# An attention pair on one core: one output group per 16 steps at a fixed place in the loop, with VectorE's small work put beside it

## The chip, the cores and the metric

The kernel runs on one core of one Trainium2 chip. What counts is the device time of that core in microseconds (us); three runs before the change gave 1822.85, 1823.55 and 1823.87 us.

## The reference

Two attention blocks over 2048 positions with 640 features and 32 heads of 20 are computed independently, and their outputs stand side by side. A looks back at 8 positions, two apart; B is full attention.

```python
def _A_ref(x, wqkv, wo):                 # H = 32, Dh = 20, W = 8, dil = 2
    ...
    q, k, v = qkv[0], qkv[1], qkv[2]
    ...
    logits = jnp.einsum("bhsd,bhswd->bhsw", q, kg) * scale
    logits = jnp.where(mask[None, None, :, :], logits, -1e9)
    attn = _softmax(logits, axis=-1)
    o = jnp.einsum("bhsw,bhswd->bhsd", attn, vg)
    return (lambda x, *d: x.transpose(*d))(o, 0, 2, 1, 3).reshape(B, S, D) @ wo

def _B_ref(x, wqkv, wo):
    ...
    scores = jnp.einsum("bhqd,bhkd->bhqk", q, k) * (Dh ** -0.5)
    p = _softmax(scores, axis=-1)
    o = jnp.einsum("bhqk,bhkd->bhqd", p, v)
    return (lambda x, *d: x.transpose(*d))(o, 0, 2, 1, 3).reshape(B, S, D) @ wo

return jnp.concatenate([a, b], axis=-1)
```

## The kernel before

The program has three stages. First TensorE makes the projections of A and B. Then comes **the loop**, which is most of the time: B's attention, with A's attention threaded through it. Last come 24 steps without maxima and B's output projection, which I call **the tail**.

**B's loop** has 512 steps (`NS`). A step is one block of 128 keys against 512 queries of four heads; 16 steps (`NKB`) make a unit, and four units a group of four heads. Per step there are four score matmuls (`s`, 512 columns, contraction 62), whose results ScalarE turns into exponentials (`e`), and four more matmuls (`m`) that give the scores transposed, from which VectorE takes row maxima (`mx`). The maxima run 24 steps (`LEAD`) ahead of the scores, so the first 488 steps have both kinds and the last 24 have scores alone. Then a step's four `P` matmuls (`e` times `vb`) add into one bank of PSUM; two steps share a bank, and ScalarE copies it out (`more`), for GpSimd to add into `braw`.

Two steps make a **pair**, written out by hand in `b_pair`, always two score or maximum matmuls at a time, in two row halves of the array. In the words of the new code the order of a pair is `P sm MM ss P sm MM ss sm sm`: `MM` are two maxima that one VectorE instruction reads (1024 elements), `sm` a score and a maximum (512 elements). So a pair has two reductions of 1024 and four of 512 on VectorE, and eight exponentials and one copy on ScalarE.

**PSUM** has eight banks, which every kind of matmul shares inside the loop. A planner chooses the bank: `pe`, `act` and `dve` carry running estimates of time (`.us`), `read_at[n]` says when bank `n` will have been read, and `b_two`, `b_pv` and `bank` take the bank that is free first by that. It decides which bank, not the order of the work.

**The other work** is queued by `after(n, fn)`, which runs `fn` n steps later, in `tick`. Every engine runs its instructions in the order in which they were written. On VectorE the small work of the loop is:

- `max_rows`: the last reduction of a unit's maxima (`mx<-mx`) and its transpose (`mtr`);
- `normalize`: a reciprocal of the sums (`sm`), which come from SyncE's DMAs `s_d<-braw` and `sm<-s_d`, and go back through `s_d<-sm` and `rb<-s_d`;
- `a_softmax`: a maximum (`am<-al`) and a reciprocal (`am<-am`) for each of A's 16 tiles of 128 rows;
- `a_turn`: five transposes (`turn<-ao`) for each tile of A's result.

**A's attention** is 128 pieces (`UNITS`), mostly on GpSimd; `next(a_work)` does one. 23 of them stand ahead of the loop. In the loop `i % 30 % 4 == 1` takes eight in 30 steps. A's **output groups** (`a_out`: 15 matmuls `ww,aot` of 320 columns and one copy `ro`; two per tile, 32 in all) are started by `out_piece` at every sixth step, between the halves of a pair, if one is ready. B's own output groups (`out_group`, 15 matmuls `ww,xn`/`ww,xl`) for all but the last quarter of the queries wait in the list `fill`, which is popped once per pair.

The lines that do this in the loop:

```python
        if i > 14 and i % 30 % 4 == 1 and next(a_work, 0) == 0:
...
        if done_a and done_a[0][0] <= 0 and i % 8 == 7 and i > 14:
            a_turn(*done_a.pop(0)[1:])
...
        if fill:
            fill.pop(0)()
        elif i % 6 == 5 and not out_piece() and not left_a[0] and not WO_b:
            load_out(wo_b, WO_b)
```

Nearly all instructions are recorded by one helper, so that the profile gives them one line, L60; they are told apart by their tiles.

Of the kernel before, what the change touches and what calls it, by code (L numbers as in the profile page):

```python
# [12 lines left out]
ALU = mybir.AluOpType  # L13
AX = mybir.AxisListType
# [7 lines left out]
KC = 5  # L22
# [18 lines left out]
NKB = 16  # L41
# [23 lines left out]
def attention_pair(ctx, tc, xa, wqk_a, wv_a, wo_a, xb, wqk_b, wv_b, wo_b, oa, ob):  # L65
# [14 lines left out]
        due.setdefault(now[0] + n, []).append((fn, args))  # L80

    loop = [None]

    def odd(n):

# [10 lines left out]
    pair = [0]  # L96
    taken = {}
    read_at = []

    def bank():  # L100

        if read_at:
            n = one(pe.us)
            pe.us = max(pe.us, read_at[n]) + 2.2
# [245 lines left out]
    def a_scores(t, c, kv):  # L350
# [7 lines left out]
            pool(kv[:, :, :n], kv[:, :, :n], kv[:, :, n:2 * n], ALU.add)  # L358
        pool(L[:, 2 * c:2 * c + 2], kv[:, :, :H], kv[:, :, 4 * H:5 * H], ALU.add)

    def a_softmax(t):

        _, L, _ = a_t[t]
        if t % (NT // 2) == 0:
            pool(L, L, mask, ALU.add)
        yield
        yield
        m = sb.tile([128, 4, H], F32, tag="am", bufs=2, name="am")
        dve.tensor_reduce(m[:, 0], L.rearrange("p o h -> p h o"), AX.X, ALU.max)
        yield  # L370
        pool(L, L, m[:, 0].unsqueeze(1).to_broadcast([128, WIN, H]), ALU.subtract)
        yield
        yield
# [5 lines left out]
        yield  # L379
        dve.reciprocal(m[:, 0], m[:, 0])  # L380
        yield
        pool(L, L, m[:, 0].unsqueeze(1).to_broadcast([128, WIN, H]), ALU.mult)

    def a_values(t, c, kv):
# [15 lines left out]
    def a_attention():  # L400
        for n in range(2):
            a_fetch(n)
        soft = {}
        for n, (t, c) in enumerate(UNITS):
            a_fetch(n + 2)
            for g in soft.values():
                next(g, None)
            if c == 4:
                for _ in soft.pop(t):
# [12 lines left out]
            next_a[0] = n + 1  # L422
            yield
# [165 lines left out]
    def max_rows(m4, m1, q, qc):  # L589
# [2 lines left out]
        md = dr.tile([2, GH * 512], F32, tag="mdr", bufs=4, name="mdr")  # L592
        raw = mt[:, 0].bitcast(F32)

        def turn():

            dve.transpose(raw, m1)
# [13 lines left out]
        t = odd(1)  # L611
        after(t, dve.tensor_reduce, m1[:, :16], m4.rearrange("p r a c -> p (r a) c"), AX.X, ALU.max)
        after(t, turn)
        after(t + 1, parts)
        after(t + 3, store)
        after(t + 4, load)

    def normalize(raw, g, c0, t, then):

        sm = sb.tile([128, 16], F32, tag="sm", bufs=2, name="sm")  # L620
        s_d = dr.tile([2, GH, 512], F32, tag="s_d", bufs=4, name="s_d")
        rb = sb.tile([128, 512], F32, tag="rb", bufs=2, name="rb")

        def bcast():
            for j in range(GH):
                sp.dma_start(rb[32 * j:32 * j + 32], s_d[1, j].partition_broadcast(32))

        def out():
            for j in range(GH):
                r0 = (g * GH + j) * DH  # L630
                sp.dma_start(ot_b[r0:r0 + DH, c0:c0 + 512], raw[32 * j:32 * j + DH])
        after(t, sp.dma_start, s_d[0], raw[DH:128:32])
# [3 lines left out]
        after(t + 1, sp.dma_start, s_d[1].rearrange("j (p c) -> j p c", c=16), sm)  # L636
        after(t + 2, bcast)
        after(t + 4, pool, raw, raw, rb, ALU.mult)
        after(t + 8, out)
        if then:  # L640
            after(t + 9, then)

    mxt = {}
    m1s = [sb.tile([128, 32], F32, tag=f"mx1{n}", bufs=1, name="mx1") for n in range(2)]
# [1 line left out]
        gp.memset(t, 0.0)  # L646

    def max_tiles(i):
        u, sub = divmod(i, NKB)
        if sub == 0:  # L650
# [14 lines left out]
    def max_end(i):  # L665
        u, sub = divmod(i, NKB)
        if sub == NKB - 1:
            max_rows(*mxt[u], stacks[u // NQC][0], u % NQC)

    def b_max(i):  # L670
# [39 lines left out]
                    give(ps2[r])  # L710

    exp_at = {}
    behind_v = [False]

    def b_pv(i):
        u, kb = divmod(i, NKB)
# [37 lines left out]
    def b_two(what):  # L754

        t = pe.us + 0.129 * behind_v[0]
        lag = 0.53 if behind_v[0] else 0.44
# [30 lines left out]
    def b_pair(i, pv):  # L788

        m = i + LEAD  # L790
        max_tiles(m)
        s = [("s", i + j, pl, r) for j in range(2) for pl in range(2) for r in range(2)]
        pv(i - LAG)
        b_two([s[0], ("m", m, 0, 1)])
        b_two([("m", m, 1, 0), ("m", m, 1, 1)])
        b_two([s[1], s[2]])
        yield
        pv(i - LAG + 1)
        b_two([s[3], ("m", m, 0, 0)])
        b_two([("m", m + 1, 0, 0), ("m", m + 1, 0, 1)])  # L800
        yield
        b_two([s[4], s[5]])
        b_two([s[6], ("m", m + 1, 1, 1)])
        b_two([s[7], ("m", m + 1, 1, 0)])
        max_end(m + 1)


    outs_b = {}
# [48 lines left out]
        after(1, sp.dma_start, vb_d[s * 128:(s + 1) * 128, half * 16 * VC:half * 16 * VC + c], ve[:, :c])  # L857


    V_GROUPS = [(n, half, s) for n in (2, 3, 0, 1) for half in range(2) for s in range(4 * n, 4 * n + 4)]  # L860
    v_late = V_GROUPS[-LAG:]
    for n, half, s in V_GROUPS[:-LAG]:
# [16 lines left out]
            next(a_work, None)  # L879
        if groups in (26, 28):  # L880
            v_piece(0, *((0, 4) if groups == 26 else (8, 16)))
    tick()
    after(4, v_piece, 0, 4, 8)
    wait[0] = 2
    WO, loads = [], []

    def load_out(src, W, halves=range(2)):
        for h in halves:
            w, more = wide_pieces(src[h], gp)
            W.append(w)  # L890
            loads.extend(more)
    load_out(wo_a, WO, (0,))
    assert next(steps, None) is None


    outs = iter(())
# [12 lines left out]
    read_at += 8 * [0.0]  # L909
    for e in (pe, act, dve):  # L910
        e.us = 0.0
    for i in range(NS + LAG):
        g, sub = divmod(i, NQC * NKB)
        if sub == 4 and g + 1 < NG:
# [14 lines left out]
        if i + LEAD >= NS:  # L929

            read_at.clear()
            if i < NS:
                b_qk(i)
            if i % 2:
                b_pv(i - LAG - 1)
                b_pv(i - LAG)
                if fill:
                    fill.pop(0)()
            continue
        if i % 2 == 0:  # L940
            steps = b_pair(i, b_pv if i else lambda _: v_group(*v_late.pop(0)))
        next(steps)
        if i % 2 == 0:
            continue
# [4 lines left out]
        if fill:  # L949
            fill.pop(0)()  # L950
        elif i % 6 == 5 and not out_piece() and not left_a[0] and not WO_b:
            load_out(wo_b, WO_b)
        next(steps, None)


    qc = NQC - 1
# [54 lines left out]
```

## Time and profile before

| What | us |
|---|---|
| median of three runs | 1823.55 |
| the profiled execution: its span, from the first to the last instruction | 1820.8 |
| difference of the two | 2.75 |
| VectorE busy over the span | 1337.7 |
| ScalarE busy | 1327.9 |
| GpSimd busy | 1219.7 |
| TensorE busy with matmuls, as modelled | 1802.5 |

For the profiled execution no time is given beside its span, so the table sets the median of the runs against it. The loop's 244 pairs lie between 448.93 and 1711.27 us: I number them from 0 and let each begin with the start of its first maximum on VectorE. The granted clock of TensorE is 1.00 in every window of the loop and the tail.

### The profile page before, as it was taken

What the parts mean: (1) busy time and instruction counts of PE and PEld (TensorE: products, weight loads), DVE (VectorE), ACT (ScalarE), POOL (GpSimd) and SP (SyncE); (2) the same over time, 40 slices, a digit from 0 to 9 for tenths busy, and PEclk for the clock granted to TensorE, in tenths of its full rate; (3) what the DMA queues carried; (4) which work ended last, traced back from release to release, by engine and by line L of the source; (5) the groups of instructions that cost most, each with busy time, mean ns of one, the idle gap of its engine ahead of it and who ended that gap; (6) DMA issues with size and microseconds to landing.
All of it is one profiled execution on the core that took longest, in us unless ns stands there. A gap on an engine that the chain in (4) does not pass through costs nothing. (4 is left out here: it accounts for less than half of the span.)

```text
span 1820.8 us, 31714 instructions
## 1 busy us (share of the span) xinstructions
PE 1802.5 (99%) x11211; PEld 997.1 (55%) x11211; DVE 1337.7 (73%) x1838; ACT 1327.9 (73%) x2597; POOL 1219.7 (67%) x1072
## 2 busy tenths in 40 slices
PE   9999999999999999999999999999999999999999
PEld 8888888877344444444343444444444444443568
DVE  3100232357999999999999899999999999999400
ACT  4222322212998888998989889889998999899892
POOL 0000068856689889999989989899999973346232
PEclk9999999999999999999999999999999999999999
DMA  6323696874443444354435335353543441121023
GB/s 227 112 94 108 193 311 247 275 246 142 127 145 111 131 131 124 119 146 138 116 106 154 116 115 130 112 146 103 154 129 121 109 116 53 40 67 55 28 74 110
DMA packets 193015, 240.31 MB, mean 132 GB/s; under 512 B 90972, under 2 KB 121308, under 8 KB 191864
## 3 DMA queue, kind: packets, MB, share of 16 engines
q1 hardware_dynamic: 192280, 237.63, 43.1%
q8 instruction: 88, 1.44, 0.3%
q10 hardware_dynamic: 576, 0.66, 0.1%
q14 instruction: 71, 0.58, 0.1%
HBM read 173.29 MB, written 64.91 MB: 131 GB/s over the span
## 5 line engine op out<-in xcount | busy, mean ns | idle before, releaser
L60 DVE TENSOR_REDUCE mx<-ps_st 128x1 f32<-128x512 f32 (+1 forms) x1512 | 1216.0, 869 | 95.3 <-PE ps_st L60 92.1
L60 ACT ACTIVATE e<-ps_st 128x512 f32<-128x512 f32 x2048 | 1063.2, 611 | 54.6 <-PE ps_st L60 36.3
L60 PE MATMUL ps_st<-bq,bk 62*128 62x512 f32 x2048 | 629.4, 443 | 1.1 <-ACT e L60 0.5
L60 PE MATMUL ps_st<-bk,bq 60*128 60x512 f32 x2048 | 594.5, 441 | 7.5 <-DVE mx L60 4.2
L60 PEld LDWEIGHTS ps_st<-bq,bk 62*128 62x128 f32 x2048 | 286.1, 184 | 523.1 <-ACT e L60 296.7
L60 PE MATMUL ps_st<-e,vb 128*32 128x512 f32 x4096 | 542.9, 604 | 3.0 <-ACT e L60 2.8
L60 POOL TENSOR_TENSOR braw<-braw,more 128x512 f32<-128x512 f32 x224 | 287.6, 1284 | 199.6 <-ACT more L60 196.1
L60 POOL TENSOR_TENSOR akv<-akv,aq 128x1280 f32<-128x1280 f32 x64 | 189.0, 2953 | 239.5 <-DMA akv<-ka_d 239.5
L60 PEld LDWEIGHTS ps_st<-bk,bq 60*128 60x128 f32 x2048 | 273.6, 184 | 51.1 <-DVE mx L60 23.6
L60 POOL TENSOR_TENSOR akv<-akv 128x640 f32<-128x640 f32 (+3 forms) x304 | 284.5, 936 | 23.8
L60 ACT COPY ro<-ps_st 128x480 f32<-128x480 f32 (+1 forms) x124 | 61.3, 496 | 237.2 <-PE ps_st L60 182.7
L60 PEld LDWEIGHTS ps_st<-e,vb 128*32 128x32 f32 x4096 | 82.1, 108 | 159.4 <-issue 99.8
L60 POOL TENSOR_TENSOR akv<-akv,al 128x1280 f32<-128x1280 f32 x64 | 152.1, 2377 | 13.2 <-DMA bq<-qb_d 7.0
L60 PE MATMUL ps_st<-wc,xn 128*128 128x480 f32 x576 | 135.8, 380 | 0.2 <-ACT xn L60 0.2
L60 ACT COPY more<-ps_st 128x512 f32<-128x512 f32 x224 | 132.8, 593 | 2.0 <-PE ps_st L60 1.8
L60 PE MATMUL ps_st<-ww,xn 128*128 128x320 f32 x768 | 129.5, 319 | 1.6 <-ACT ww L60 1.1
L60 PEld LDWEIGHTS ps_st<-ww,xn 128*128 128x128 f32 x768 | 116.0, 192 | 23.3 <-ACT e L60 9.2
L60 PEld LDWEIGHTS ps_st<-wc,xn 128*128 128x128 f32 x576 | 107.9, 188 | 18.0 <-ACT xn L60 0.8
L60 PE MATMUL ps_st<-xn,w 128*128 128x512 f32 x480 | 115.8, 390 | 0.0
L60 PEld LDWEIGHTS ps_st<-xn,w 128*128 128x128 f32 x480 | 90.1, 188 | 19.3
L60 ACT CAST pr<-ps_st 128x512 fp32r<-128x512 f32 x40 | 23.6, 589 | 100.9 <-PE ps_st L60 100.9
L60 DVE TENSOR_TENSOR pr<-ps_st,pr 128x512 fp32r<-128x512 f32 x40 | 27.7, 692 | 91.4 <-ACT pr L60 91.4
(64 smaller groups left out, 995.8 us busy)
## 6 DMA issues: line engine op xcount, KB each, us to landing
akv<-ka_d SPq DMA_DIRECT2D x128, 320.0 KB
akv<-va_d SPq DMA_DIRECT2D x128, 320.0 KB
kb_d<-pr SPq DMA_DIRECT2D x20, 512.0 KB
qb_d<-pr SPq DMA_DIRECT2D x20, 512.0 KB
bk<-kb_d SPq DMA_DIRECT2D x16, 640.0 KB
bq<-qb_d SPq DMA_DIRECT2D x64, 160.0 KB
rb<-s_d SPq DMA_DIRECT2D x128, 64.0 KB
stg<-xb SPq DMA_DIRECT2D x12, 512.0 KB
```

The costliest lines, as they stand in the source:

```text
L60: return self.tc.keep_in_program_order(op(*a, **k))
```

## The change

The pair's order becomes data. `PAIR` is the order of before. `BESIDE` is used for one pair of eight, the one with `i % 16 == 8`; it begins with `G`, one of A's output groups ahead of the pair's own scores, and has its two `P` together. Right behind the group's matmuls `flush` writes all of VectorE's small work that has come due since the last such place (`beside`). After step 452 `G` does two groups. A's pieces come at `i % 4 == 3`, four in 16 steps. `a_turn` writes its five transposes together instead of one per step, and at most once per 16 steps. B's output groups are not taken inside the loop any more. The first tile of A is turned, and the first half of A's output weights loaded, ahead of the loop. `small` gives the planner a stated time for each small instruction, and `bank` counts the switch from `P`.

```diff
+    PAIR = "P sm MM ss P sm MM ss sm sm".split()
+    BESIDE = "G ss sm MM sm P P ss sm MM sm".split()
+    def b_pairs(pv, group):
+        scores = ((i, pl, r) for i in range(NS - LEAD) for pl in range(2) for r in range(2))
+        maxima = ((m, j) for m in range(LEAD, NS) for j in range(2))
...
+        for i in range(0, NS - LEAD, 2):
+            for t in BESIDE if i % NKB == NKB // 2 else PAIR:
+                if t == "P":
+                    yield
+                    pv(next(steps))
+                elif t == "G":
+                    group()
...
+    def small(us, op, *args):
+        t = dve.us
+        op(*args)
+        dve.us = t + us
...
+    def flush():
+        while beside:
+            op = beside.pop(0)
+            (small if len(op) > 1 else op[0])(*(op if len(op) > 1 else ()))
+    def group():
+        for _ in range(2 if now[0] - loop[0] > NS - 60 else 1):
+            out_piece()
+        flush()
...
         for k in range(KC):
-            after(1 + k, dve.transpose, b[:, k], o[:, k * 128:(k + 1) * 128])
-        after(KC + 2, sp.dma_start, d, b.rearrange("p k c -> p (k c)"))
-        after(KC + 5, back)
+            small(0.27, dve.transpose, b[:, k], o[:, k * 128:(k + 1) * 128])
+        after(2, sp.dma_start, d, b.rearrange("p k c -> p (k c)"))
+        after(5, back)
...
+        def turn():
+            small(0.24, dve.reciprocal, sm, sm)
+            after(1, sp.dma_start, s_d[1].rearrange("j (p c) -> j p c", c=16), sm)
+            after(2, bcast)
+            after(4, pool, raw, raw, rb, ALU.mult)
+            after(8, out)
...
-        t = odd(t + 3)
-        after(t, dve.reciprocal, sm, sm)
+        if now[0] - loop[0] < NS - LEAD - NKB // 2 - 4:
+            after(t + 3, beside.append, (turn,))
+        else:
+            after(t + 3, turn)
...
-            normalize(raws.pop(u), g, qc * 512, 2 if last else 5, (lambda: out_last(qc)) if last else None)
+            normalize(raws.pop(u), g, qc * 512, 2 if last else 3, (lambda: out_last(qc)) if last else None)
...
-        if i > 14 and i % 30 % 4 == 1 and next(a_work, 0) == 0:
+        if i > 14 and i % 4 == 3 and next(a_work, 0) == 0:
             for d in done_a:
                 d[0] -= 1
-        if done_a and done_a[0][0] <= 0 and i % 8 == 7 and i > 14:
-            a_turn(*done_a.pop(0)[1:])
+        if i % NKB == NKB // 2 - 1 and done_a and done_a[0][0] <= 0:
+            beside.append((lambda d=done_a.pop(0): a_turn(*d[1:]),))
...
+        if groups == 14:
+            a_turn(*done_a.pop(0)[1:])
```

VectorE, before, over some two pairs in the middle of the loop (`128x1` is a reduction of 512 elements, `128x2` one of 1024; the number behind `mx` is the buffer of one unit's maxima, and `mx_2531` the unit's last reduction):

```order
L60 TENSOR_REDUCE mx_4445<-ps_st 128x2
L60 TENSOR_REDUCE am<-al 128x32
L60 TENSOR_REDUCE mx_4445<-ps_st 128x1
L60 TENSOR_REDUCE mx_4445<-ps_st 128x2
L60 TENSOR_REDUCE mx_4445<-ps_st 128x1 x2
L60 TENSOR_REDUCE mx_4911<-ps_st 128x1
L60 TENSOR_REDUCE mx_4911<-ps_st 128x2
L60 RECIPROCAL sm<-sm 128x16
L60 TENSOR_REDUCE mx_2531<-mx_4445 128x16
L60 STREAM_TRANSPOSE mtr<-mx_2531 128x32
L60 TENSOR_REDUCE mx_4911<-ps_st 128x1
```

And after, at one of the new places:

```order
L60 TENSOR_REDUCE mx_4935<-ps_st 128x2
L60 TENSOR_REDUCE mx_4935<-ps_st 128x1 x2
L60 RECIPROCAL am<-am 128x32
L60 RECIPROCAL sm<-sm 128x16
L60 STREAM_TRANSPOSE turn<-ao 128x128 x5
L60 TENSOR_REDUCE mx_2532<-mx_4935 128x16
L60 STREAM_TRANSPOSE mtr<-mx_2532 128x32
L60 TENSOR_REDUCE mx_5388<-ps_st 128x1
L60 TENSOR_REDUCE mx_5388<-ps_st 128x2
```

The small work has moved into one block at the boundary between two units' maxima. These nine instructions stand there in every second block; in the others the block is `am<-al`, `sm<-sm`, `mx<-mx` and `mtr`, four instructions.

TensorE, before, around one of A's output groups (`bq,bk` are scores, `bk,bq` maxima, `e,vb` a `P`, `ww,aot` the group):

```order
L60 MATMUL ps_st<-e,vb 32x512 x4
L60 MATMUL ps_st<-bq,bk 128x512
L60 MATMUL ps_st<-bk,bq 128x512 x3
L60 MATMUL ps_st<-ww,aot 128x320 x15
L60 MATMUL ps_st<-bq,bk 128x512 x3
L60 MATMUL ps_st<-bk,bq 128x512
L60 MATMUL ps_st<-bq,bk 128x512
L60 MATMUL ps_st<-bk,bq 128x512
L60 MATMUL ps_st<-e,vb 32x512 x4
```

And after, around the same kind of group:

```order
L60 MATMUL ps_st<-bq,bk 128x512
L60 MATMUL ps_st<-bk,bq 128x512
L60 MATMUL ps_st<-ww,aot 128x320 x15
L60 MATMUL ps_st<-bq,bk 128x512 x3
L60 MATMUL ps_st<-bk,bq 128x512 x3
L60 MATMUL ps_st<-bq,bk 128x512
L60 MATMUL ps_st<-bk,bq 128x512
L60 MATMUL ps_st<-e,vb 32x512 x8
L60 MATMUL ps_st<-bq,bk 128x512 x3
L60 MATMUL ps_st<-bk,bq 128x512 x3
```

The group has moved from the middle of a pair to its head, and the pair's two `P` have come together behind its first four scores. The loop has 30 such places, eight pairs apart; the last two have two groups each (`x30`).

More of the change, by code (lines that the diff above doesn't have):

```diff
@@ L82, in attention_pair, with in_place @@
     loop = [None]
+    beside = []
+    def small(us, op, *args):
+        t = dve.us
+        op(*args)
+        dve.us = t + us
+    def in_place(n, *ops):
+        if loop[0] is None:
+            for op in ops:
+                after(n, small, *op)
+        else:
+            after(n, beside.extend, ops)
     def odd(n):
@@ L408, in a_attention @@
             if c == 4:
+                late.add(t)
                 for _ in soft.pop(t):
@@ L610, in load @@
                              md[:, r * 1024:(r + 1) * 1024].rearrange("t (p c) -> t p c", p=2))
[L611 to L616, printed above, removed]
+        def turn():
+            small(0.17, dve.tensor_reduce, m1[:, :16], m4.rearrange("p r a c -> p (r a) c"), AX.X, ALU.max)
+            small(0.21, dve.transpose, raw, m1)
+            after(1, parts)
+            after(3, store)
+            after(4, load)
+        if loop[0] is None:
+            after(1, turn)
+        else:
+            beside.append((turn,))
     def normalize(raw, g, c0, t, then):
@@ L857, in v_group, with load_out @@
         after(1, sp.dma_start, vb_d[s * 128:(s + 1) * 128, half * 16 * VC:half * 16 * VC + c], ve[:, :c])
+    WO, loads = [], []
+    def load_out(src, W, halves=range(2)):
+        for h in halves:
+            w, more = wide_pieces(src[h], gp)
+            W.append(w)
+            loads.extend(more)
     V_GROUPS = [(n, half, s) for n in (2, 3, 0, 1) for half in range(2) for s in range(4 * n, 4 * n + 4)]
@@ L881, in attention_pair @@
             v_piece(0, *((0, 4) if groups == 26 else (8, 16)))
+        if groups == 14:
+            a_turn(*done_a.pop(0)[1:])
+        turn_parts()
+        if groups == 28:
+            wait[0] = 2
+            load_out(wo_a, WO, (0,))
+        if loads and groups >= 28:
+            loads.pop(0)()
     tick()
     after(4, v_piece, 0, 4, 8)
[L884 to L893, printed above, removed]
+    assert next(steps, None) is None and not loads
     outs = iter(())
@@ L911, in attention_pair @@
         e.us = 0.0
+    def flush():
[6 more added lines that the diff above has]
+        flush()
+    steps = b_pairs(lambda i: b_pv(i) if i >= 0 else v_group(*v_late.pop(0)), group)
+    next(steps)
     for i in range(NS + LAG):
@@ L948, in attention_pair @@
             spare += [sb.tile([128, 2, 512], F32, tag="last0", bufs=2, name="more") for _ in range(2)]
[L949 to L953, printed above, removed]
+        if i < NS - LEAD:
+            next(steps, None)
+            if not left_a[0] and not WO_b:
+                load_out(wo_b, WO_b)
+            continue
+        read_at.clear()
+        flush()
+        if i < NS:
+            b_qk(i)
+        if i % 2:
+            b_pv(i - LAG - 1)
+            b_pv(i - LAG)
+            if fill:
+                fill.pop(0)()
     qc = NQC - 1
```

121 lines of the change are left out of this document (65 added, 56 removed).

## The prediction

> **What bounds the kernel now.** I read the page's first part, then the windows over the loop, then VectorE's groups of instructions in the loop, then who waits for whom, and last single pairs.
>
> ```profile
> PE 1802.5 (99%) x11211; PEld 997.1 (55%) x11211; DVE 1337.7 (73%) x1838; ACT 1327.9 (73%) x2597; POOL 1219.7 (67%) x1072
> 448.93:1711.27 1262.34, 1253.12 (x8335) 543.21 (x8332) 1191.43 (x1661) 1139.91 (x2245) 1018.85 (x888) 1.00 0.40 114
> ```
>
> The second row is the loop: 1262.34 us, then the busy time of PE, PEld, DVE, ACT and POOL. VectorE (DVE) is busy for 1191.43 us, 94%; ScalarE (ACT) for 1139.91 us. The loop is bound by VectorE, with 71 us in which it stands still. VectorE's work there, and its waits:
>
> ```profile
> L60 DVE TENSOR_REDUCE mx<-ps_st 128x1 f32<-128x512 f32 x972 | 627.6, 679 | 66.7 <-PE ps_st L60 63.5
> L60 DVE TENSOR_REDUCE mx<-ps_st 128x2 f32<-128x1024 f32 x486 | 590.6, 1215 | 0.0
> L60 DVE STREAM_TRANSPOSE turn<-ao 128x128 f32<-128x128 f32 x80 | 23.4, 293 | 0.0
> L60 DVE TENSOR_REDUCE am<-al 128x32 f32<-128x256 f32 x13 | 7.9, 610 | 0.0
> L60 DVE RECIPROCAL sm<-sm 128x16 f32<-128x16 f32 x30 | 7.2, 240 | 0.0
> L60 DVE STREAM_TRANSPOSE mtr<-mx 128x32 f32<-128x32 f32 x30 | 6.3, 212 | 1.2
> L60 DVE TENSOR_REDUCE mx<-mx 128x16 f32<-128x64 f32 x31 | 5.2, 169 | 0.0
> L60 DVE RECIPROCAL am<-am 128x32 f32<-128x32 f32 x13 | 4.2, 326 | 1.1 <-POOL am L60 1.1
> DVE mx L60 <- PE ps_st L60: 65.5, 81, 1.9
> ACT ro L60 <- PE ps_st L60: 66.0, 35, 2.5
> L60 ACT COPY ro<-ps_st 128x320 f32<-128x320 f32 x35 | 15.0, 427 | 66.0 <-PE ps_st L60 66.0
> ```
>
> Two things matter here. The small work (the last six DVE rows) is 23.4 + 7.9 + 7.2 + 6.3 + 5.2 + 4.2 = 54.2 us. And VectorE's 65.5 us of waiting for TensorE belong to the output groups: ScalarE waits 66.0 us for its 35 copies `ro`, one behind each group (32 of A's, so 3 of B's). One such place:
>
> ```profile
> 833.79 2.47 PE L60 MATMUL ps_st<-ww,aot 128*128 128x320 f32 x15
> 836.30 0.43 ACT L60 COPY ro<-ps_st 128x320 f32<-128x320 f32 x1 [1.90 <-PE ps_st L60]
> 836.99 1.29 DVE L60 TENSOR_REDUCE mx<-ps_st 128x1 f32<-128x512 f32 x2 [1.48 <-PE ps_st L60]
> 838.77 1.82 DVE L60 TENSOR_REDUCE mx<-ps_st 128x1 f32<-128x512 f32 x2 [0.49 <-PE ps_st L60]
> ```
>
> The group takes TensorE 2.4 us (the next matmul starts at 836.19). VectorE runs out of filled banks, stands for 1.48 us, and for 0.49 us once more behind the next `P`: 1.97 us with nothing to do. The small work lies elsewhere, where VectorE has none to spare.
>
> I then cut the loop into its 244 pairs (each from its first maximum to the next pair's) and asked for windows on them; the first column is the length:
>
> ```profile
> 448.93:455.17 6.24, 6.24 (x43) 3.95 (x41) 4.52 (x6) 4.71 (x10) 0.94 (x2) 1.00 0.65 189
> 469.30:474.30 5.00, 4.81 (x35) 1.81 (x32) 4.96 (x9) 4.71 (x9) 3.48 (x5) 1.00 0.56 149
> 479.02:483.93 4.91, 4.47 (x34) 1.66 (x32) 4.91 (x7) 4.63 (x9) 1.48 (x2) 1.00 0.91 253
> 533.82:540.57 6.75, 6.75 (x49) 3.98 (x47) 5.13 (x7) 4.97 (x11) 6.59 (x5) 1.00 0.11 31
> 540.57:545.41 4.84, 4.84 (x36) 2.04 (x33) 4.53 (x6) 4.84 (x10) 4.53 (x7) 1.00 0.45 142
> 981.38:986.04 4.66, 4.66 (x34) 1.62 (x34) 4.66 (x7) 4.60 (x9) 4.50 (x4) 1.00 0.82 275
> 986.04:990.94 4.90, 4.46 (x34) 1.66 (x32) 4.90 (x7) 4.63 (x9) 4.82 (x4) 1.00 0.89 253
> 990.94:995.86 4.92, 4.92 (x35) 2.01 (x31) 4.70 (x7) 4.70 (x10) 4.84 (x4) 1.00 0.12 39
> 995.86:1000.79 4.93, 4.93 (x36) 2.12 (x33) 4.75 (x7) 4.72 (x9) 4.77 (x4) 1.00 0.44 151
> 1592.44:1599.13 6.69, 6.69 (x47) 3.65 (x45) 5.07 (x7) 4.66 (x10) 2.53 (x2) 1.00 0.17 55
> 1599.13:1603.97 4.84, 4.84 (x36) 2.00 (x34) 4.52 (x6) 4.84 (x10) 1.28 (x1) 1.00 0.57 171
> 1666.05:1671.11 5.06, 4.91 (x36) 1.85 (x34) 4.97 (x9) 4.76 (x9) 2.44 (x4) 1.00 0.35 112
> 1685.60:1690.53 4.93, 4.93 (x36) 2.11 (x33) 4.75 (x7) 4.73 (x9) 2.04 (x2) 1.00 0.00 0
> ```
>
> - A pair with one of A's groups and no small work: 23 of them, first and last at 533.82 and 1592.44, mean **6.74**.
> - The pair behind it, without small work: 18, at 540.57 to 1599.13, mean **4.84**; here ScalarE is busy throughout and catches up.
> - A pair with small work: 67, at 469.30 to 1666.05, mean 5.12 for 0.61 us of small work. So that work is mostly paid in full.
> - An undisturbed pair, the second or later behind a group or a small instruction: 70, at 479.02 to 1685.60, mean **4.77**. The shortest kind, directly behind a small instruction, is 4.66 (981.38), where VectorE never waits. The longest come in runs: 4.90, 4.92, 4.93 from 986.04 on, where ScalarE and TensorE wait for each other's banks.
>
> **The change, part by part.**
>
> *The block at the group.* The order shows two kinds of block, taking turns: `am` maximum, `sm`, `mx`, `mtr`, that is 0.61 + 0.24 + 0.17 + 0.21 = 1.23 us; and `am` reciprocal, `sm`, five transposes, `mx`, `mtr`, 0.33 + 0.24 + 5 x 0.293 + 0.38 = 2.41 us. Both begin when VectorE has read the last filled bank, which is where it stood still for 1.97 us. The first fits; of the second 0.44 us stick out. So a group pair should take 6.74, or 6.74 + 0.44 = 7.18. Ends: nothing sticks out (6.74), or only the 1.48 us gap counts (2.41 - 1.48 = 0.93, so 7.67). I take the middle, since the same pair holds both gaps.
>
> *The pairs without it* lose their small work and become undisturbed ones: 4.77, with 4.66 and 4.92 as ends.
>
> *Two `P` together.* They save TensorE a switch, but starve both readers for the length of a second `P`. Apart, a `P` takes 1.00 us until the next matmul starts:
>
> ```profile
> 1006.62 1.06 PE L60 MATMUL ps_st<-e,vb 128*32 128x512 f32 x8
> 1007.62 0.49 PE L60 MATMUL ps_st<-bq,bk 62*128 62x512 f32 x1
> 1008.54 1.04 PE L60 MATMUL ps_st<-e,vb 128*32 128x512 f32 x5
> ...
> 1712.79 1.92 PE L60 MATMUL ps_st<-e,vb 128*32 128x512 f32 x16
> 1714.64 2.03 PE L60 MATMUL ps_st<-ww,xn 128*128 128x320 f32 x12
> ```
>
> The upper end is a second 0.49 us gap in each of 30 places, +14.7; the lower end is 30 times 0.15 saved, -4.5, since in the tail, where two stand together (1712.79), they take 1.85. Four scores and four maxima stand ahead of them now, about 2.5 us for VectorE (two reductions at 627.6/972 and one at 590.6/486), so I take 0.
>
> *Waits that it adds.* `flush` makes VectorE wait in place for whatever a small instruction needs, with all later maxima behind it, and then TensorE for the banks. The likeliest is `sm`, whose DMAs now start three steps behind `P` instead of five, and whose instruction comes 3.5 pairs, 3.5 x 4.77 = 16.7 us, behind it. In the tail, with nothing to hide it, the chain from ScalarE's copy to the reciprocal is 7.4 us:
>
> ```profile
> 1779.62 0.59 ACT L60 COPY more<-ps_st 128x512 f32<-128x512 f32 x1 [1.54 <-PE ps_st L60]
> 1786.98 0.26 DVE L60 RECIPROCAL sm<-sm 128x16 f32<-128x16 f32 x1 [3.36 <-DMA sm<-s_d]
> ```
>
> Nine us of cover remain for GpSimd's and SyncE's queues, so nothing. If the cover were gone, each microsecond would cost 30 us over the 30 places. The `am` operations have four steps, two pairs, or more behind GpSimd's part, some 9.5 us; the transposes' input is older still.
>
> *A's pieces*, 4 in 16 steps instead of 8 in 30, give GpSimd a little less to do per step; it was busy for 1018.85 of 1262.34 us. Nothing, as long as A ends in the loop, and the order has its last group there. Five transposes ahead of the loop are 1.5 us at most, beside a TensorE stage: nothing.
>
> *B's three groups* leave the loop for the tail, where TensorE has no gap and a group takes 1788.47 - 1786.28 = 2.19 us:
>
> ```profile
> 1720.00:1740.00 20.00, 20.00 (x144) 13.19 (x140) 0.00 (x0) 17.71 (x37) 5.11 (x4) 1.00 0.15 48
> 1786.28 1.92 PE L60 MATMUL ps_st<-ww,xn 128*128 128x320 f32 x12
> 1788.47 1.92 PE L60 MATMUL ps_st<-ww,xn 128*128 128x320 f32 x12
> ```
>
> That is 3 x 2.19 = +6.6 us (0 if the tail had slack; 7.4 at a group's 2.47).
>
> **The sum.** 15 x 6.74 + 15 x 7.18 = 208.8 for the pairs with a group. The last two places have a second group: 2 x 2.19, less the 0.44 that it covers, 3.9. 30 x 4.84 = 145.2 behind them. The first pair keeps its 6.24. The other 183 pairs at 4.77 are 872.9. Together 1237.0 against 1262.3: -25.3 in the loop, +6.6 in the tail, **-18.7**. The profiled span of 1820.8 becomes 1802.1; the runs' median lies 2.75 above the span, which I carry over: **1805 us**.
>
> **The rivals.** What decides is the undisturbed pair: each 0.01 us of it is 1.83 us. No change lies at 4.77 + 18.7/183 = 4.872.
>
> - *The bank order settles in the slow kind of pair; slower.* Place: the seven pairs between two groups, where nothing disturbs the planner's rotation any more. Price: 183 x (4.92 - 4.77) = +27.5, so 1832. It decides from 4.872 on. For it: the 4.9s come in runs, and far behind a disturbance (986.04, 1685.60); small work is what led back to 4.66. Against it: the mean of 70 such pairs.
> - *The pairs settle at VectorE's own pace* of 4.66: 183 x 0.11 = -20.1, and with all blocks hidden -6.6 more: 1778. For it: VectorE is busy throughout at 981.38. Against it: that pair stands directly behind small work, when its banks are full.
> - *The block isn't covered*: VectorE comes to it late or waits in it, so that all of it is paid. 15 x 1.23 + 15 x (2.41 - 0.44) = +48, so 1853. Against it: the gap at 836.99 and the 9 us of cover.
> - *TensorE is the bound*, and hiding VectorE's work brings nothing: the loop stays, the tail adds 6.6, so 1830. For it: PE is busy for 1253.12 of 1262.34 us. Against it: from 1006.62 to 1008.54 it does half a pair's `P` and three of the eight other steps in 1.92 us when banks are free, so a pair in 2 x 1.92 + 2 x 0.31 = 4.46, which is under 4.66. The Trainium skill (Perfetto Trace Analysis, Identifying the Most-Contended Engine) says that matmul busy time does not measure how near TensorE is to its limit, since pipelined instructions show otherwise than they run, and that weight loads are a better sign. By matmul busy time the loop could shorten by 9.2 us at most. The trace agrees with the page: PEld is busy for 543.21 us, 43%.
>
> **How the numbers follow.** Forecast (undisturbed pairs between 4.70 and 4.85, 1792 to 1820): 0.52. Faster rival: 0.18. Slow pairs: 0.16. Uncovered block: 0.08. TensorE: 0.06. A run can tell about 0.2%, 3.6 us, from no change. Faster by more: nearly all of the forecast and the second rival, 0.68. Within: a little of the forecast and half of the slow pairs, 0.11. Slower: the rest, 0.21. The range leaves out the uncovered block, the far half of the faster rival and the end of the slow pairs: 1783 to 1830. The forecast's own range is 1792 to 1820.
>
> **What would show it.** In the changed profile: VectorE's wait for TensorE in the loop falls from 65.5 us to under 30; its small instructions stand behind no idle time; pairs with a group take 6.7 and 7.2 in turn, the next 4.84, the others 4.77; the tail grows by 6.6 us. I am wrong if VectorE waits at `sm` or `am`, if undisturbed pairs are above 4.87, or if ScalarE waits longer than 66 us for `ro`, since no part of the change gives ScalarE anything to do there.

## The result, and the profile after

The changed kernel takes 1806.21 us (median; 1804.68 to 1807.87) where the kernel before took 1823.20 on the same chip: a ratio of 0.9907, with an interval of 0.9893 to 0.9921. That is 17.0 us faster. The prediction was 1805, with 0.68 on faster. The profiled execution has a time of its own here, 1806.6 us, beside its span of 1804.8.

The windows by pairs, here as in the kernel before, begin 0.24 us ahead of the start of the first maximum that the timeline shows (449.77 for the loop here); the same holds for the other runs' windows, so no length is changed by it.

The engines' busy time over the span, and the window over the loop (length; then PE, PEld, DVE, ACT and POOL busy, the granted clock, DMA share and GB/s), after:

```profile
PE 1779.3 (99%) x11211; PEld 984.3 (55%) x11211; DVE 1344.6 (75%) x1838; ACT 1329.4 (74%) x2597; POOL 1222.7 (68%) x1072
449.53:1687.46 1237.93, 1222.75 (x8288) 523.81 (x8284) 1195.62 (x1656) 1140.99 (x2244) 1023.27 (x890) 1.00 0.41 115
```

| Stage, us | before | after | forecast |
|---|---|---|---|
| ahead of the loop | 448.9 | 449.5 | 448.9 |
| the loop | 1262.3 | 1237.9 | 1237.0 |
| the tail | 109.5 | 117.3 | 116.1 |

The loop is 24.4 us shorter and VectorE does the same work in it, so it is now busy for 96.6% of it. Two rows tell where the time came from, VectorE's and ScalarE's waits for TensorE in the loop (us in total, times, longest); a third row has grown:

```profile
DVE mx L60 <- PE ps_st L60: 34.9, 60, 3.2
ACT ro L60 <- PE ps_st L60: 35.5, 31, 1.8
ACT more L60 <- PE ps_st L60: 18.2, 29, 0.6
```

VectorE waits for 34.9 us instead of 65.5. One of the new places in the timeline of after (start, length, what; in brackets the idle time before it), with the larger block:

```profile
952.95 2.44 PE L60 MATMUL ps_st<-ww,aot 128*128 128x320 f32 x15
954.54 0.34 DVE L60 RECIPROCAL am<-am 128x32 f32<-128x32 f32 x1
954.80 0.20 DVE L60 RECIPROCAL sm<-sm 128x16 f32<-128x16 f32 x1
954.91 1.02 DVE L60 STREAM_TRANSPOSE turn<-ao 128x128 f32<-128x128 f32 x5
955.42 0.43 ACT L60 COPY ro<-ps_st 128x320 f32<-128x320 f32 x1 [1.15 <-PE ps_st L60]
955.85 0.18 DVE L60 TENSOR_REDUCE mx<-mx 128x16 f32<-128x64 f32 x1
956.06 0.21 DVE L60 STREAM_TRANSPOSE mtr<-mx 128x32 f32<-128x32 f32 x1
956.20 2.38 DVE L60 TENSOR_REDUCE mx<-ps_st 128x1 f32<-128x512 f32 x3
959.16 7.13 DVE L60 TENSOR_REDUCE mx<-ps_st 128x1 f32<-128x512 f32 x9 [0.58 <-PE ps_st L60]
```

The block starts at 954.54, and the first new maximum at 956.20 follows with no idle time: the group's time on TensorE is filled. One gap is left, 0.58 us behind the two `P`. The block with `am<-am` is also shorter than I had added up, 1.66 us: the recorded durations run into the start of the next instruction, and the five transposes take 1.02 us instead of 5 x 0.293.

Cut into pairs as before, after's windows read (a group with the larger block, the pair behind it, six undisturbed pairs in one row; then the next group, with the smaller block, and the pair behind it):

```profile
949.59:955.96 6.37, 6.29 (x45) 4.13 (x43) 6.37 (x15) 5.13 (x11) 5.98 (x7) 1.00 0.55 142
955.96:961.26 5.30, 5.30 (x42) 1.79 (x40) 4.68 (x8) 4.55 (x10) 2.47 (x4) 1.00 0.29 87
961.26:989.88 28.62, 28.20 (x194) 10.87 (x192) 28.40 (x37) 27.64 (x54) 26.07 (x22) 1.00 0.60 164
989.88:996.10 6.22, 6.22 (x43) 4.08 (x41) 6.03 (x11) 5.05 (x11) 5.72 (x5) 1.00 0.02 5
996.10:1001.48 5.38, 5.38 (x42) 2.02 (x40) 4.51 (x6) 4.60 (x9) 3.86 (x5) 1.00 0.21 57
```

In the first row VectorE is busy for all of 6.37 us. By these windows the group and the block lie at the end of one pair, and the pair behind it is the one whose scores and `P` the code writes from `BESIDE`. Over 28 regular periods the pair with the group takes 6.30, the one behind it 5.35, the other six 4.70 to 4.87 each (in the third row 28.62 / 6 = 4.77). A period is 40.33 us; in the kernel before eight pairs took 41.39 on average over the loop.

The tail grew by more than B's three groups. Windows of after around the end of the loop, and on the whole tail:

```profile
1668.55:1671.97 3.42, 3.42 (x28) 1.37 (x27) 3.42 (x5) 3.30 (x7) 3.34 (x3) 1.00 0.36 107
1671.97:1675.38 3.41, 2.58 (x15) 0.92 (x14) 3.26 (x4) 3.16 (x7) 3.33 (x4) 1.00 0.14 35
1675.38:1678.79 3.41, 3.41 (x22) 1.03 (x14) 3.16 (x5) 1.55 (x3) 1.97 (x3) 0.54 0.11 33
1685.62:1689.03 3.41, 2.07 (x14) 1.01 (x16) 2.51 (x5) 2.93 (x7) 1.28 (x4) 1.00 0.27 76
1689.03:1692.44 3.41, 3.41 (x17) 0.77 (x10) 0.00 (x0) 2.95 (x7) 1.06 (x1) 0.54 0.00 0
1687.46:1804.80 117.34, 113.53 (x783) 85.45 (x783) 5.43 (x12) 68.15 (x140) 34.90 (x33) 0.99 0.25 80
```

TensorE's granted clock, 1.00 in every such window before, falls to half for 3.4 us twice (0.54 in the third row and the fifth, which begin 0.24 us ahead of the falls at 1675.62 and 1689.27), each time behind a window in which TensorE is busy for only 2.58 or 2.07 us.

### The profile page after: what moved, and what is told of

Its sections match the earlier page's. It is cut to its first block, busy times and chain, and to the rows that moved or that the text cites. A ratio compares the mean times of both kernels' runs of the same rounds, so it can differ in the third digit from the quotient of the medians.

```text
span 1804.8 us, 31644 instructions
## 1 busy us (share of the span) xinstructions
PE 1779.3 (99%) x11211; PEld 984.3 (55%) x11211; DVE 1344.6 (75%) x1838; ACT 1329.4 (74%) x2597; POOL 1222.7 (68%) x1072
## 4 chain that ended last, share of the span: by engine, by line
PE 78%; DVE 18%; DMA 2%; ACT 1%; issue 1%; SPq 0%; POOL 0%; ACTq 0%; POOLq 0%
PE ps_st L60 78%; DVE mx L60 18%; ACT e L60 1%; DMA bq<-qb_d 1%; DMA stg<-wv_b 1%; DMA bk<-kb_d 0%; DVE xl L60 0%; SPq L60 0%; DVE pr L60 0%; ACT pr L60 0%; ACT xl L60 0%; POOL ident L60 0%; ACT ro L60 0%; DVE sm L60 0%; ACTq L60 0%
## 5 line engine op out<-in xcount | busy, mean ns | idle before, releaser
L60 PE MATMUL ps_st<-bq,bk 62*128 62x512 f32 x2048 | 620.3, 443 | 1.8 <-DVE mx L60 1.3
L60 PE MATMUL ps_st<-bk,bq 60*128 60x512 f32 x2048 | 583.9, 442 | 9.1 <-DVE mx L60 4.4
L60 PEld LDWEIGHTS ps_st<-bk,bq 60*128 60x128 f32 x2048 | 267.6, 184 | 46.2 <-DVE mx L60 23.7
L60 PE MATMUL ps_st<-xn,w 128*128 128x512 f32 x480 | 115.8, 390 | 0.0
```

What stands on the lines that cost most here:

```text
L60: return self.tc.keep_in_program_order(op(*a, **k))
```

## The experiments

Two theories stood at the start. *Cover*: the gain is VectorE's small work filling the time of a group. *Order*: the gain is the pair's new order and even pace, and where the small work stands hardly matters.

### Taking the cover away

Each of A's output groups is cut to one of its 15 matmuls, in the kernel before (`b_cut`) and in the changed one (`a_cut`), so that hardly a gap is left to fill.

```diff
-                p = bank()
-                rows15(p, lambda xi, k: ot[:, xi, k], W[half])
+                p = bank(0.3)                     # the planner's time for a group, 2.2 before
+                pe.matmul(p[:, :320], ot[:, 0, 0], W[half][0][:, 0], start=True, stop=True)
```

> The kernel before, with one matmul in place of the 15 in each of A's 32 output groups in the loop; this leaves most of A's output projection out. Theory 'cover' (the change gains because VectorE's small work now runs while TensorE does an output group) and its rival 'order' (the gain comes from the group's fixed place and the steadier order of pairs and banks, wherever the small work stands) expect the same here: a group costs a pair 6.74 - 4.77 = 1.97 us and the pair behind it little, nothing else is hidden beside it, so 32 x 2.0 = 64 us less, about 1759.

> The changed kernel with the same cut, which leaves the same part of A's output projection out. 'Cover': without the long group the 54 us of small work lose what hides them and come onto VectorE's path, at about the 0.68 us per us that they cost before, 30 x 1.74 x 0.68 = 36 us; so the cut brings 64 - 36, some 28 us, about 1778, slower than the same cut of the kernel before by 10 to 20 us or no faster than it. 'Order': the cut brings the same 64 us as before, about 1742, and the lead of 17 us stays.

Each of the two was measured once. Before falls to 1770.19 us, by 52.7 (64 was expected); the changed kernel to 1773.14, by only 33.1. The lead of 17.0 us is gone: 3.0 us of loss stand in its place. The windows over the loop, of `b_cut` and then of `a_cut`:

```profile
450.09:1658.93 1208.84, 1195.43 (x7887) 484.61 (x7884) 1187.59 (x1661) 1140.00 (x2245) 1017.73 (x888) 1.00 0.42 119
```

```profile
448.94:1654.04 1205.10, 1178.64 (x7840) 467.37 (x7836) 1192.45 (x1656) 1135.82 (x2244) 1022.23 (x890) 1.00 0.42 118
```

The second loop is shorter by 3.7 us, but B's three groups, some 6 us, still stand in the first alone. With no group to hide behind, a block costs what scattered work does: a fixed place alone doesn't give the gain. The cut also takes away what the order behind a long group may be worth, so it doesn't tell the theories apart by itself; the next run keeps group and order.

`a_away` keeps everything, but writes the block one pair behind the group.

```diff
+    BEHIND = ["F"] + PAIR                      # "F" calls flush()
-            for t in BESIDE if i % NKB == NKB // 2 else PAIR:
+            for t in BESIDE if i % NKB == NKB // 2 else BEHIND if i % NKB == NKB // 2 + 2 else PAIR:
...
             out_piece()
-        flush()
```

> The changed kernel with the same block of small work written one pair later, at the head of the pair behind the group's, all else alike. 'Cover': the group pair keeps its length, since TensorE sets it, with VectorE idle in it again; the pair behind has 0.6 us idle and takes the rest of 1.23 or 2.0 us, so 30 x 1.0 = 30 us more, about 1836. 'Order': within 5 us of the changed kernel, 1806.

1845.86 us, a ratio of 1.0129 (1.0112 to 1.0146): 39.7 us slower than the change. Its windows on a group's pair and on the pair with the block:

```profile
965.62:971.91 6.29, 6.21 (x43) 4.11 (x41) 5.04 (x7) 5.04 (x10) 5.97 (x5) 1.00 0.59 158
971.91:979.02 7.11, 7.05 (x54) 2.49 (x50) 6.18 (x14) 6.26 (x13) 2.85 (x3) 1.00 0.27 77
```

The group's pair is as long as with the block, but VectorE is busy for 5.04 of 6.29 us. The next pair takes 7.11 instead of 5.30, so a block one pair too late is paid in full, 1.81 us here for a block of 1.66. Over 28 periods the two pairs take 13.05 us instead of 11.66, which makes 39 of the 40.2 us by which the loop grows; 30 were expected. The loop also has five falls of the clock, but its 180 undisturbed pairs are longer by only 0.015 us on average (4.792), 2.7 us in all.

### How much fits

All transposes of A's result are made twice, before (`b_double`) and in the change (`a_double`):

```diff
+            for _ in range(2):
-                small(0.27, dve.transpose, ...)
+                small(0.27, dve.transpose, ...)   # a_double; b_double repeats the `after` line
```

> The kernel before with each of the loop's 80 transposes written twice (the second does the same again). 'Cover' and 'order' alike: small work costs about 0.68 us per us where it stands, 80 x 0.29 x 0.68 = 16 us more, about 1839.

> The changed kernel with each transpose written twice: 1.0 to 1.4 us more in every second block. 'Cover' with room left: the pair and the next are TensorE's, VectorE has 0.6 us idle in the next pair, so at most half is paid, 15 x 0.6 = 9 us or less. 'Cover' with no room: VectorE is busy all 6.37 us of that pair, so all of it is paid, 15 x 1.1 = 17 us. 'Order' expects the same cost per us as in the kernel before, 75 x 0.2 x 0.68 = 10 us, or 16 as there.

Before loses 22.0 us (ratio 1.0122, 1.0107 to 1.0137), the change 11.9 (0.9973 of before, 0.9964 to 0.9983). The added work: 160 transposes of 0.308 (the median in the first row, of `b_double`; minimum, median and maximum in ns) instead of 23.4 us are 25.9 more; in `a_double` ten in a block take 2.75 us instead of 1.02, and 15 times that is 25.9 too.

```profile
L60 DVE STREAM_TRANSPOSE turn<-ao x160: 252/308/316, 489.6 to 1556.7; 128x128 f32<-128x128 f32 x160
```

```profile
961.72 2.75 DVE L60 STREAM_TRANSPOSE turn<-ao 128x128 f32<-128x128 f32 x10
956.39:964.51 8.12, 8.04 (x59) 4.69 (x59) 7.95 (x20) 6.88 (x14) 6.61 (x7) 1.00 0.45 120
964.51:969.13 4.62, 3.82 (x28) 1.32 (x22) 4.59 (x8) 2.92 (x7) 2.74 (x4) 1.00 0.62 170
```

The loops grow by 21.2 and 9.8 us: 0.82 us is paid per microsecond of scattered work, 0.38 at the group. The windows of `a_double` show how: the group's pair grows by all 1.75 us, but the pair behind it falls from 5.30 to 4.62, since its own gap had been the one not yet filled. So about 0.7 us of room was left beside the larger block.

### The two `P` together

`a_nopp` puts the group ahead of the old order of a pair. `g_apart` keeps the scores first, but moves the two `P` apart (it stands on `a_gp`, below, 4.3 us faster than the change).

```diff
-    BESIDE = "G ss sm MM sm P P ss sm MM sm".split()
+    BESIDE = ["G"] + PAIR                              # a_nopp
+    BESIDE = "G ss sm MM sm P ss sm P MM sm".split()   # g_apart
```

> The changed kernel with the pair of the group in the common order behind the group (P sm MM ss P sm MM ss sm sm), so the two P stand apart again. Both theories leave this open. If TensorE sets the 11.66 us of the group pair and the next, the order costs or saves no more than the switch, 30 x 0.15 = 4.5 us more at most. If the double P's 0.6 us of standing still in VectorE is what makes the next pair 5.36, parting them saves up to 30 x 0.5 = 15 us. If the first scores behind the group matter because the readers are empty then, P first adds about a P, 1.0 us, less what it takes away later: 10 to 30 us more.

> The changed kernel with the last split on GpSimd (1801.9 us) and, in the pair with the group, the scores first as in the change but its two P apart: G ss sm MM sm P ss sm P MM sm. With P right behind the group and the two apart the changed kernel took 1823.4. 'Scores first': what counts is that the readers, empty behind a group, get banks before the first P; then this stays within 5 us of 1802, or is faster by the 0.6 us that VectorE stands still behind the double P, up to 15 us. 'Two together': what counts is the spared switch or the longer run of eight matmuls; then it loses much of the 17 us, about 1815.

Neither theory had this one: `a_nopp` takes 1823.40 us, ratio 1.000 (0.9991 to 1.001). The whole gain is gone. Its window on a group's pair, and its timeline there:

```profile
956.38:963.44 7.06, 6.97 (x49) 4.10 (x47) 6.65 (x16) 5.03 (x10) 6.67 (x8) 1.00 0.43 107
962.12 1.07 PE L60 MATMUL ps_st<-e,vb 128*32 128x512 f32 x8
962.22 0.43 ACT L60 COPY ro<-ps_st 128x320 f32<-128x320 f32 x1 [1.15 <-PE ps_st L60]
963.64 1.57 ACT L60 ACTIVATE e<-ps_st 128x512 f32<-128x512 f32 x3 [0.99 <-PE ps_st L60]
963.68 13.17 DVE L60 TENSOR_REDUCE mx<-ps_st 128x1 f32<-128x512 f32 x16 [0.61 <-PE ps_st L60]
```

Directly behind the group comes a `P`, with no new scores between them: ScalarE stands for 1.15 and then 0.99 us, VectorE for 0.61. In the change ScalarE's first gap is the same 1.15, but four scores come before the `P`. Over 28 periods of `a_nopp` the group's pair takes 7.04 and the one behind it 4.83, together 0.22 us more than 6.30 + 5.35, or 6.6 over 30. The larger part is in the other pairs: their mean is 4.845 instead of 4.777, which over 180 pairs is 12.2. Its last three pairs are 2.0 us shorter. That is 16.8, as much as its loop is longer than the change's (1254.8 to 1237.9).

`g_apart` takes 1816.37, 14.5 over `a_gp`: the group's pair and the next take 6.49 + 5.60 = 12.09, 0.44 more, or 13 over 30; the other pairs stay at 4.78. Of the 20.8 us by which `a_gp` is faster than the kernel before, `g_apart` keeps 7.0. So the two `P` together shorten the group's two pairs, and scores first alone are not the gain; by what means they do isn't shown, since the spared switch was priced at 0.15 us a place. What holds the others at 4.78 is common to the change and `g_apart`, and `a_nopp` lacks it: scores and maxima ahead of the first `P` behind a group. How that reaches pairs several places later is not shown.

`g_allpp` (on `a_gp` too) gives every pair the two `P` together:

```diff
-    PAIR = "P sm MM ss P sm MM ss sm sm".split()
+    PAIR = "ss sm MM sm P P ss sm MM sm".split()
```

> The same kernel with every pair in the order of the group's pair (ss sm MM sm P P ss sm MM sm), the group's as in the change. 'Two together': TensorE is spared a switch per pair, 0.15 us, and the pairs go towards VectorE's 4.66: up to 20 us faster, about 1782. 'Scores first': it helps behind a group alone, and elsewhere the double P only makes the readers run dry, 0.1 to 0.5 us in each of 214 pairs: 20 to 100 us slower.

1968.15 us, 1.0793 (1.0776 to 1.081), 166 over `a_gp` where 100 was the most expected. Six of its plain pairs:

```profile
1031.54:1064.85 33.31, 33.28 (x194) 14.93 (x193) 28.46 (x37) 27.10 (x55) 25.74 (x22) 1.00 0.52 141
```

A pair takes 5.55 us, 0.77 more, with VectorE idle for 4.85 of 33.31 us: here the second `P` starves the readers as the prediction's upper end had it (0.49 us), and by more. Together they pay only behind a group.

### The planner and the pace

`a_plan` takes out what the change tells the planner; `a_pace` takes A's pieces at the old steps.

```diff
-            n = one(pe.us + 0.2)
-            pe.us = max(pe.us + 0.2, read_at[n]) + 2.2
-            behind_v[0] = True
+            n = one(pe.us)
+            pe.us = max(pe.us, read_at[n]) + 2.2
...
-        dve.us = t + us                                  # a_plan: up to here
...
-        if i > 14 and i % 4 == 3 and next(a_work, 0) == 0:
+        if i > 14 and i % 30 % 4 == 1 and next(a_work, 0) == 0:   # a_pace alone
```

> The changed kernel with the planner's part of the change undone alone: no stated times for the small instructions, and the group's bank and the switch behind it reckoned as before. The order of work on every engine is the same; only banks differ. If the undisturbed pairs' length (4.78 in the change, 4.85 with P first) is a matter of the bank rotation, it moves by 0.02 to 0.1 us in 180 pairs, 4 to 18 us either way. If it isn't, within 3 us of 1806.

> The changed kernel with A's pieces at the old pace alone, eight in 30 steps. Both theories: GpSimd has room either way and the blocks stay at their place, so within 3 us of 1806. If the even pace matters, since pieces at changing distances from the block make it wait or miss it, 5 to 20 us slower.

`a_plan`: 1806.23 us, the change's time. `a_pace`: 1828.10 (1.0027, 1.0013 to 1.0041), the whole gain and 5 us more; its ten runs lie at 1824 to 1826 and at 1830 to 1833, and the profile, of 1830.33, is of the second kind. Its periods with a smaller block are as in the change, 40.27 us; the loss sits in twelve pairs that take over 0.45 us more than the change's, together 24.9 us more; the longest has 13.14 us instead of 4.71. From its timeline there:

```profile
1467.90 1.26 POOL L60 TENSOR_TENSOR braw<-braw,rb 128x512 f32<-128x512 f32 x1 [6.04 <-DMA mdr<-mtr]
1469.88 0.42 ACT L60 ACTIVATE al<-al 128x256 f32<-128x256 f32 x1 [5.62 <-POOL al L60]
1470.82 0.79 PE L60 MATMUL ps_st<-bk,bq 60*128 60x512 f32 x1 [5.54 <-ACT more L60]
1471.59 0.35 DVE L60 RECIPROCAL am<-am 128x32 f32<-128x32 f32 x1 [6.92 <-POOL am L60]
```

This reciprocal stands two pairs behind the block's place: its tile's piece came before the next place, so `a_softmax` wrote the rest of its chain at once (`late`). GpSimd waits for a DMA, ScalarE for GpSimd, TensorE for ScalarE, and VectorE for GpSimd's next step. The change has one such late reciprocal too, in a pair of 4.86 us that is not longer than others. Two more of the twelve, of 7.74 and 7.63 us, hold a block in which VectorE waits in place for the sums, 1.23 and 1.11 us, as it never does in the loop of the change:

```profile
965.71 0.25 DVE L60 RECIPROCAL sm<-sm 128x16 f32<-128x16 f32 x1 [1.11 <-DMA sm<-s_d]
```

Eight of the other nine stand four to eight pairs behind one of the three blocks with such a wait (the third is 0.53 us), four of them with a fall of the clock inside. How the old pace brings the wait, and the wait those pairs, is not shown.

### Two versions meant to be faster

In the changed kernel TensorE waits at the end of the loop behind VectorE's last copy of B's output rows (`xl`):

```profile
1672.22 1.62 DVE L60 TENSOR_TENSOR xl<-stg,xl 128x512 fp32r<-128x512 f32 x1 [0.15 <-ACT xl L60]
1674.49 0.50 PE L60 MATMUL ps_st<-bk,bq 60*128 60x512 f32 x1 [0.77 <-DVE mx L60]
```

`a_gp` gives that step to GpSimd for all but the last quarter of the queries.

```diff
+        g = ("stg", gp, gp.tensor_copy) if qc < NQC - 1 else ()
-        split(chunk(o, 0, k), chunk(o, 1, k), ot_b[...])
+        split(chunk(o, 0, k), chunk(o, 1, k), ot_b[...], *g)
```

> The changed kernel with the last split of B's result for the first three quarters of the queries on GpSimd instead of ScalarE and VectorE. In the changed kernel this stands in pair 241 (6.76 us) and TensorE's granted clock falls to 0.5 for 3.4 us just behind it (pair 242: 6.00 us). If VectorE's and ScalarE's instructions make TensorE wait there and the wait brings the lower clock, pairs 241 and 242 take 4.8 each and the clock stays 1.0: 3 us less, about 1803. If the wait has another cause, or the clock falls by itself, nothing changes.

1801.87 us, 0.9885 of before (0.9871 to 0.99), the fastest version. The two pairs that took 6.76 and 6.00 us, in `a_gp`:

```profile
1669.48:1674.21 4.73, 4.73 (x36) 1.94 (x32) 4.73 (x7) 4.59 (x9) 4.57 (x5) 1.00 0.25 71
1674.21:1679.07 4.86, 4.86 (x38) 2.08 (x34) 4.86 (x7) 4.61 (x10) 4.70 (x6) 1.00 0.17 39
```

The granted clock there is 1.00 again. The other fall, at the loop's end, stays.

`a_split` makes each group in two parts, 9 and 6 matmuls, four pairs apart, holding its bank between.

```diff
+    OTHER = ["H"] + PAIR          # "H": the rest of a group, at i % 16 == 0
-                rows15(p, lambda xi, k: ot[:, xi, k], W[half])
+                rows15(p, o, W[half], range(3))
+                read_at[taken[id(p)][0]] = 1e9        # the bank stays taken
+                yield
+                rows15(p, o, W[half], range(3, KC))
```

> The changed kernel with each output group in two parts, 9 matmuls at the old place and 6 matmuls four pairs later, the bank held between. If what costs 2.1 us per group is that it is longer than the filled banks last, two short parts cost nearly nothing and VectorE, small work included, sets the time: 8 x 4.66 + 1.74 = 39.0 instead of 40.35 us per 16 steps, 30 x 1.3 = 40 us less, about 1766. If a bank held for half the time costs as much as it brings, within 10 us of 1806; slower if seven banks don't carry the pairs: 0.1 us for each of 120 pairs is 12 us more.

1886.01 us, 1.0344 (1.0326 to 1.0361). Over the periods the pair with the first part takes 6.11 us, the three behind it, with the bank held, 5.69, 5.33 and 5.28, the pair with the second part 6.37, and the three with the bank back 4.83, 4.85 and 4.80. In the change the first five are 6.30, 5.35, 4.71, 4.70 and 4.82. So seven banks in place of eight cost 0.3 to 0.6 us in a pair, and as much again lies in the pair with the second part, which is 1.55 us longer where the first part saves 0.19.

## Why the prediction was right, and where it was not

**The number** came out to 1.2 us, and that is in part luck. The span was forecast at 1802.1 us and is 1804.8; the 2.75 us carried over from span to time are 1.8 in the profiled execution, where both are known, which hides 0.95 of the miss. And one term was wrong and was made good by another. The loop, 0.9 over the forecast, comes apart like this: the pairs with a group and those behind them -3.5 (28 x 11.66 + 27.9 for the two places with two groups = 354.4, forecast 208.8 + 3.9 + 145.2 = 357.9), 180 undisturbed pairs at 4.777 +1.2, the last three pairs, behind the `xl` steps, +3.1 (6.76 + 6.00 + 4.68 instead of 3 x 4.77), and the first pair +0.1.

**The block at the group** is covered, as said: `b_cut`, `a_cut` and `a_away` show it. The part of 0.44 us that was to stick out is not there: the pair with the larger block is 0.13 us longer than that with the smaller, 6.37 to 6.24. Two terms were mis-sized: five transposes are 1.02 us instead of 1.47, since the recorded 0.293 counts the overlap with the next instruction, and VectorE's second gap no longer lies in the group's pair but in the next. So 6.74, 7.18 and 4.84 became 6.24, 6.37 and 5.35; in pairs of two the forecast of 11.80 was 0.14 too long.

**Two `P` together**, which I took as 0 between -4.5 and +14.7, is the step that failed. With the two apart and the scores still first the kernel loses 14.5 us (`g_apart`), and with the old order in that place it is no faster than before (`a_nopp`): the term is -14.5, or -17 for the whole order, outside its bounds either way. I compared a double `P` with two single ones, and not what stands behind the group: in `a_nopp` a `P` there lets both readers run dry. Part of it went through the undisturbed pairs. I took their 4.77 from the kernel before as given, but `a_nopp`, with the same small work moved, has 4.845. That is the direction of the rival of slow pairs, and 0.03 below the point where it was to take the whole gain; with its longer group pairs nothing was left. So under the old order the rest of the sum, -18.7 in the forecast, is worth nothing; that this error and the one in the order cancel to 1.2 us is luck.

**Waits that it adds** came out at nothing, but that rests on a condition I passed over: A's even pace, also costed at nothing. With the old pace `a_pace` loses 21.9 us, and VectorE then waits in place at `sm` in three blocks, the sign that I had named, and once at a late `am`; the three long pairs that hold such a wait make 11.1 of the 24.9 us. At `sm` and `am` the change itself doesn't wait, as forecast.

**The tail**: +7.8 instead of +6.6. The difference goes with the fall of the clock at the loop's end: the two runs that have B's three groups in the tail and no such fall, `a_nopp` and `a_away`, have tails of 115.8 and 115.3, so the groups are 5.8 to 6.3; the nine with the groups and the fall have 117.1 to 117.4 (3.4 us at half speed are 1.7 us of work at most).

**TensorE as the bound** fell as argued: by matmul busy time the loop could have lost 9.2 us, and it lost 24.4. The rule of the Trainium skill (Perfetto Trace Analysis, Identifying the Most-Contended Engine) agrees with that.

**Signs.** The small instructions stand behind no idle time: right. VectorE's wait of under 30 us: 34.9, a near miss. Groups at 6.7 and 7.2: wrong. Undisturbed pairs at 4.77: right. ScalarE's wait at `ro`, for which I saw no cause to change, fell from 66.0 to 35.5 us: the group now starts while ScalarE still has exponentials to do, 1.15 us of idle time ahead of `ro` instead of 1.90, and 18.2 us of waiting stand at `more` now, behind the double `P` (1.8 over the whole kernel before).

## What to carry to other kernels

When one engine's long block starves the bound engine, put that engine's odd jobs exactly there, and look at what the first engine does right after the block. Here its next work had to feed the starved readers, and its accumulations had to stand together behind that: with neither the gain was gone (`a_nopp`), and with the first alone two thirds of it (`g_apart`, 7.0 of 20.8 us left). The place of the block and the order behind it were each worth the whole gain, and one pair too late turned it into a loss. A fixed place also needs its inputs to arrive evenly, since an engine that runs in order waits in place for a late one.

## What the runs showed of the hardware

**The granted clock goes by fixed windows.** Within each trace the falls to half begin whole multiples of 3.413 us apart (in `a_away` 81, 98, 49, 25 and 49 of them lie between one and the next), and end on the same raster. The five 3.41 us windows of the changed kernel above lie 0.24 us ahead of it. In fourteen traces I counted TensorE's matmul starts in each such window, from 470 us on to 30 us before the end: of 21 windows with 12 or fewer, 19 were followed by a window at half clock; of 69 with 13 or 14, 3; of some 5,360 with 15 or more, none. The rest of the changed kernel's loop has 17 or more in each. No single long gap is needed: TensorE's longest is 0.77 us ahead of the first fall in the changed kernel, and `a_away` has five falls with none over 0.5. The Trainium skill (TensorE: Matmul & The Clock Gate, HAM oscillation) gives as its rule no idle gaps of TensorE over some 3.4 us; these traces agree with the length, but the falls come without such a gap. Its next section (A second HAM failure mode: psum-queue depth-cycling) tells of short idle times that bring the clock to half and back; these traces fit that, with 0.19 us the longest idle time ahead of a fall in `a_away`, but what they show is the number of starts.

**Transposes** of 128x128 on VectorE are recorded with 0.293 us scattered and 0.266 in a block, but the next instruction begins earlier, 0.215 us behind a scattered one and 0.193 behind one in a block (medians of the starts, `before` and `after`), so that five take 1.02 us. When each is made twice into the same place, the ten take 2.75 us (`a_double`), 0.275 each.
